# Half of the sequence rows of a Fourier mix from mirrored PSUM banks, with the mirrored input and output carried through DRAM

## The chip, the cores and the metric

The kernel runs on one core of a Trainium2 chip. The core has five engines, each with an instruction queue of its own that is worked off in order: TensorE (PE in the profile; its weight loads are listed as PEld), VectorE (DVE), ScalarE (ACT), GpSimd (POOL) and SyncE (SP). SP, ACT and POOL can also start DMA transfers; an instruction that starts one is shown as SPq, ACTq or POOLq. The metric is the device time of one execution in microseconds (us), as the median of several runs.

## The reference

Two parts, one after the other. The inputs are q, k and v of shape (4, 8, 768, 64), 8 memory keys and values for each head, and two MLP weights, 512x2048 and 2048x512. The result is (4, 768, 512) in fp32.

```
# attention: chunks of 32 queries see 16 keys to the left, 8 to the right and 8 memory keys
scores = scale * q_c @ concat(mem_k, k[l_start:r_end]).T
x[:, c_start:c_end] = softmax(scores) @ concat(mem_v, v[l_start:r_end])
# Fourier mix and MLP
mixed = real(fft(fft(x, axis=1), axis=2))          # over 768 rows and 512 columns
u  = x + mixed
un = (u - mean(u)) / sqrt(var(u) + 1e-6)
out = u + relu(un @ w_ch1) @ w_ch2
```

The input is real, so the real part of the two-dimensional transform has a symmetry that the change uses: `mixed[768 - r, 512 - c] = mixed[r, c]`, with indices taken modulo 768 and 512. Rows 0 and 384 are their own mirror images.

## The kernel before

**Units of work.** There are four batches. Each has four pairs of heads, 16 pairs in all (`attention(n)`, n from 0 to 15), then a Fourier stage (`first_fourier` for batch 0, `fourier(b)` for the others, both ending in `columns_of`), then an MLP in two halves of 384 rows (`mlp`). A batch's x lies in SBUF as `xsb`, six row tiles of 128 rows by 512 columns in fp32. Three batches have room for it.

**Attention.** GpSimd loads q and k (line 286), SP loads v with seven DMAs a pair (lines 299 to 305) into one of four buffers `va`. PE transposes q and k, forms scores and multiplies by v (lines 313, 351, 372); ACT does the exponentials (359); DVE divides by the sum and writes `xsb` (382 and 383, called normalisation below).

**Fourier stage.** DVE folds the input along both axes (lines 400 to 431), so that only a quarter of it, in even and odd combinations, goes through PE. The row transform is `e_rows` (line 440): four pairs (`par`, `ab`) with PSUM banks `ps`. It gives 193 row frequencies of each parity. ACT writes the high fp16 half of each to `up` (`e_up`, line 452), DVE the low half (`e_rest`, line 456). `up` holds frequencies 0 to 384. For the rows above, DVE makes a copy in reversed order, `dn` (`e_dn`, line 461). The column transform is `e_columns` (line 545): for each of six row tiles `kt`, eight matmuls into one PSUM bank `pm`, two column parities of four products each, with 128x128 weights from `up` (tiles 0 to 2) or `dn` (tiles 3 to 5) and 256 columns of the tables `cosD` and `nsinD` or `sinD`. Then for each tile DVE adds `pm` to `xsb` in place (`e_sum`, line 551) and takes mean and variance (557, 558), and ACT writes the fp16 copy `un` (563). In batches 1 to 3 SP transposes `un` by DMA into `unT` (`e_flip`, line 575); in batch 0 PE and DVE do it.

**MLP.** For each half, 16 products `ph` of four matmuls (line 596), each followed by a ReLU on ACT (603), then three row tiles `pc` of 16 matmuls (610); DVE scales and adds (`e_osb`, line 616) into `osb`, of which there are three buffers, and ACT sends it out (`e_out`, line 620).

**What sets the order.** Each piece of work is a task with an engine, an estimated cost, the tasks it comes after, and the buffers that it takes and gives back. `Plan.order` is a list scheduler: it works through time and places on each engine the first task that can start, in order of rank. MLP products rank last and are called fillers: PE takes one whenever nothing else is ready. The order that comes out is fixed in the program; the engines then run it in order with their own waits. PSUM has two banks with the tag `acc` (row transforms, column transforms and, in batch 3, a third of the MLP) and two with the tag `mlp`. A task of SP that is `loose` may be placed before one that is held up.

**DMA semaphores.** DMAs that SP and ACT issue signal eight semaphores, which the program assigns in turn. An instruction that starts a DMA waits until the earlier user of its semaphore has landed.

Of the kernel before, what the change touches and what calls it, by code (L numbers as in the profile page):

```python
# [10 lines left out]
FP32 = mybir.dt.float32  # L11
BF16 = mybir.dt.bfloat16
FP16 = mybir.dt.float16
# [18 lines left out]
def strided(src, off, dims):  # L32
    return bass.AP(tensor=src.tensor, offset=src.offset + off,
                   ap=[list(src.ap[0])] + [list(d) for d in dims])
# [105 lines left out]
def kernel(  # L140
# [49 lines left out]
    seq = [(b, pr) for b in range(B) for pr in (0, 2, 1, 3)]  # L190

    plan = Plan(dict(qs=NS, ks=NS, va=NV, kTb=NKT, qT=2, tr=1, sc=1, xa=1, e1=3,
                     xsb=3, fold=2, hl=1, up=4, dn=4, acc=2, mlp=2, un=6, unT=2, hT=1, osb=3))
    add = plan.add
    MLPS = 1000000

# [189 lines left out]
            xa[:, :, :, 0:D], zs.unsqueeze(3).to_broadcast([P, 3, 2, D]), ALU.mult)  # L386


    zy_of, pq_of, ff_of, hl_of, ps_of, up_of, pm_of, un_of, tp_of = ({} for _ in range(9))
    mu_of, unT_of, rstd_of, g_of = {}, {}, {}, {}  # L390
    mid = cpool.tile([P, 2, NST, 1], FP16)
    mid32 = cpool.tile([P, NST, 1], FP32)
    warm = cpool.tile([P, 1], FP32)
    gate = cpool.tile([P, 1], FP32)

    def e_zy(b, par, c):
# [60 lines left out]
                                up[:, 0].rearrange("p k s -> p s k"), ALU.subtract)  # L457

    def e_dn(b, par, ab):
        dn = fpool.tile([P, 2, HS], FP16, tag="dn", bufs=4, name="dn")  # L460
        nc.vector.tensor_copy(dn, rev_ap(up_of[b, par, ab][2], HS, HS, [[2 * NK, 2]]))
        up_of[b, par, ab][1] = dn

    def g_zy(par, g):
        if g == 0:
# [82 lines left out]

    def e_sum(b, kt):
        uv = xs[b][:, kt, :].rearrange("p (j c) -> p c j", c=2)  # L550
        nc.vector.tensor_tensor(uv, pm_of.pop((b, kt)), uv, ALU.add)  # L551

    def e_stats(b, kt):
        if kt == 0:
# [17 lines left out]
    def e_flip(b, kt):  # L572
        if kt == 0:
            unT_of[b] = fpool.tile([P, NDT, S], FP16, tag="unT", bufs=2, name="unT")
        nc.sync.dma_start_transpose(unT_of[b][:, :, ts(kt, P)], un_of.pop((b, kt)))

    def e_unT(b, kt):
        if kt == 0:
# [3 lines left out]
    def e_rstd(b):  # L582
        rstd_of[b] = rstd = fpool.tile([P, NST], FP32, tag="rstd", bufs=2, name="rstd")
        nc.gpsimd.tensor_scalar(rstd, mu_of[b][:, :, 1], eps, None, ALU.add)  # L584
        nc.gpsimd.tensor_tensor(rstd, rstd, mhalf, ALU.pow)


    def mtag(b, i):
        return "acc" if b == B - 1 and i % 3 == 2 else "mlp"
# [21 lines left out]
                             start=(ht == 0), stop=(ht == NHT - 1))  # L611

    def e_osb(b, sh, stl):
        st = sh * 3 + stl
        osb_of[b, st] = osb = fpool.tile([P, DM], FP32, tag="osb", bufs=3, name="osb")
        nc.vector.scalar_tensor_tensor(osb, pc_of.pop((b, sh, stl)), rstd_of[b][:, st:st + 1],  # L616
                                       xs[b][:, st, :], ALU.mult, ALU.add)

    def e_out(b, st):
        nc.scalar.dma_start(out[b, ts(st, P), :], osb_of.pop((b, st)))  # L620


    t_zero = add("DVE", 0.2, e_zero, rank=-21)
    t_table = add("ACT", 1.4, lambda: nc.scalar.activation(warm, zero, AFT.Sin), [t_zero], rank=-3)
# [169 lines left out]
    def first_fourier():  # L794
# [37 lines left out]
                                              give=(tag,))  # L832
        return columns_of(0, t_rest)

    def fourier(b):
        nrm = [[t_norm[b * HP + i, g] for i in ii for g in range(2)] for ii in ((0, 1), (2, 3))]
        t_rest = {}
        zy = {}
        ff = hi = None
        for par in range(2):  # L840
            zy[par] = [None]
            for c in range(2):
                zy[par].append(add("DVE", 0.96, lambda par=par, c=c: e_zy(b, par, c),
                                   nrm[c] + [ff, zy[par][-1]],
                                   take=("fold",) if c == 0 else ()))
            pq = add("DVE", 1.86, lambda par=par: e_pq(b, par), zy[par], take=("fold",),
                     give=("fold",))
            prev = pq
            for ab in range(2):
                ff = add("DVE", 1.1, lambda par=par, ab=ab: e_ff(b, par, ab), [pq, prev],  # L850
                         take=("fold",) if ab == 0 else (), give=("fold",) if ab == 1 else ())
                prev = ff
                hi = add("ACT", 0.85, lambda par=par, ab=ab: e_hi(b, par, ab), [ff, hi],
                         take=("hl",) if ab == 0 else ())
                lo = add("DVE", 0.96, lambda par=par, ab=ab: e_lo(b, par, ab), [hi],
                         give=("fold",) if ab == 1 else ())
                rw = add("PE", 1.95 if par == 0 and ab == 1 else 1.0,
                         lambda par=par, ab=ab: e_rows(b, par, ab), [lo, t_sines],
                         take=("acc",), give=("hl",) if ab == 1 else ())
                up = add("ACT", 0.6, lambda par=par, ab=ab: e_up(b, par, ab), [rw], take=("up",))  # L860
                t_rest[par, ab] = add("DVE", 0.6, lambda par=par, ab=ab: e_rest(b, par, ab),
                                      [up], give=("acc",))
        return columns_of(b, t_rest)

    def columns_of(b, t_rest):
        t_dn = {}
        for par in range(2):
            for ab in range(2):
                t_dn[par, ab] = add("DVE", 0.36, lambda par=par, ab=ab: e_dn(b, par, ab),
                                    [t_rest[par, ab]], take=("dn",))  # L870
        t_un = {}
        allr = list(t_rest.values())
        cols = {}

        def columns(kt):
            cols[kt] = add("PE", 0.9, lambda: e_columns(b, kt),
                           allr + [t_rows] + (list(t_dn.values()) if kt > 2 else []),
                           take=("acc",), rank=len(plan.tasks) + (15 if kt == 3 else 0),
                           give=("up",) * 4 if kt == 2 else ("dn",) * 4 if kt == 5 else ())

        sa = None
        columns(0)
        for kt in range(NST):
            if kt + 1 < NST:
                columns(kt + 1)
            su = add("DVE", 0.7, lambda kt=kt: e_sum(b, kt), [cols[kt]], give=("acc",))
            sa = add("DVE", 0.9, lambda kt=kt: e_stats(b, kt), [su, sa])
            un = add("ACT", 0.72, lambda kt=kt: e_un(b, kt), [sa], take=("un",))
            if b > 0:
                t_un[kt] = add("SP", 0.1, lambda kt=kt: e_flip(b, kt), [un, t_un.get(kt - 1)],  # L890
                               take=("unT",) if kt == 0 else (), give=("un",), moved=0.8,
                               loose=True)
                continue
            tp = add("PE", 0.26, lambda kt=kt: e_turn_u(b, kt), [un, t_idh], take=("mlp",),
                     give=("un",))
            t_un[kt] = add("DVE", 0.43, lambda kt=kt: e_unT(b, kt), [tp, t_un.get(kt - 1)],
                           take=("unT",) if kt == 0 else (), give=("mlp",))
        rs = add("POOL", 1.0, lambda: e_rstd(b), [sa])
        return t_un, rs
# [3 lines left out]
    def mlp(b, t_un, rs):  # L903
        for sh in range(2):
            relu = []
            c2 = None
            for ht in range(NHT):
                ph = add("PE", 0.65, lambda sh=sh, ht=ht: e_ch1(b, sh, ht),
                         mlp_prev + [t_un[3 * sh + i] for i in range(3)] + t_w1,
                         take=(mtag(b, ht),), give=("unT",) if sh == 1 and ht == NHT - 1 else (),  # L910
                         rank=MLPS + len(plan.tasks), filler=True)
                relu.append(add("ACT", 0.5, lambda sh=sh, ht=ht: e_relu(b, sh, ht),
                                [ph, relu[-1] if relu else None],
                                take=("hT",) if ht == 0 else (), give=(mtag(b, ht),),
                                rank=RELU(len(plan.tasks))))
            for stl in range(3):
                st = 3 * sh + stl
                for part in range(4):
                    end = part == 3
                    c2 = add("PE", 0.88, lambda sh=sh, stl=stl, part=part: e_ch2(b, sh, stl, part),  # L920
                             [relu[4 * part + 3], t_w2[part], c2], take=(mtag(b, stl),) if part == 0 else (),
                             give=("hT",) if stl == 2 and end else (),
                             rank=MLPS + len(plan.tasks), filler=True)
                os_ = add("DVE", 0.76, lambda sh=sh, stl=stl: e_osb(b, sh, stl), [c2, rs],
                          take=("osb",), 
                          give=(mtag(b, stl), "xsb") if st == NST - 1 else (mtag(b, stl),),
                          rank=RELU(len(plan.tasks)))
                mlp_prev[0] = c2
                add("ACT", 0.1, lambda st=st: e_out(b, st), [os_], give=("osb",), moved=0.9,
                    rank=RELU(len(plan.tasks)))  # L930

# [46 lines left out]
```

## Time and profile before

| what | value |
|---|---|
| median of 3 runs | 309.03 us (308.47 to 309.29) |
| the profiled execution | 308.85 us |
| its span in the trace | 307.1 us |
| PE matmul busy | 94% of the span, granted clock 1.00 |
| DVE busy | 56% |
| ACT busy | 53% |
| chain that ended last | PE 91%, DMA 2%, POOL 2%, DVE 1%, ACT 1%, issue 1% |
| column transform (line 545) on that chain | 7% |
| DMA traffic | 28.93 MB, mean 94 GB/s |

The span runs from the first to the last recorded instruction or transfer; the execution's own time includes what lies around it. The "chain that ended last" is followed back from the end: at each step to what released the instruction, or to the one before it on its engine. A row of the waits names who waited, at which line, and for whom. Row times of single matmuls overlap, since matmuls are pipelined: the rate is read from the chain, where 16 of the column transform take 1.75 us.

In time the batches overlap: the column transforms of batches 0 to 3 start at about 55, 108, 147 and 202 us. From about 210 us on, the MLP of batches 1, 2 and 3 is alone.

### The profile page before, as it was taken

Reading aid. Unit: us, or ns where it says so; the run is one execution under the profiler, and the core shown is the slowest. Engines: PE = TensorE matmul, PEld = TensorE weight load, DVE = VectorE, ACT = ScalarE, POOL = GpSimd, SP = SyncE. Lnnn points to the kernel's source line nnn. Section 1 sums busy time; section 2 is a strip of 40 time slices with the busy share of each in tenths; the row PEclk is TensorE's granted clock in tenths of the full one; section 3 lists DMA queues with packets and bytes.
Section 4 is the critical chain, followed back from the end, with each engine's and each line's share of the span. In section 5 each row is a group of like instructions: output and inputs, shape, how many; then the busy total and the mean of one; then the engine's idle time right before and its main releaser. Section 6 shows DMA issues by size and latency. Waiting matters only on the chain.

```text
span 307.1 us, 7496 instructions
## 1 busy us (share of the span) xinstructions
PE 289.5 (94%) x3148; PEld 181.5 (59%) x3148; DVE 171.2 (56%) x371; ACT 161.5 (53%) x291; POOL 40.8 (13%) x78
## 2 busy tenths in 40 slices
PE   1399999999999999999989999999999999999994
PEld 1267678866666676666756646675554554554541
DVE  7877895975397887797764399476101001001001
ACT  6656373689884666885257423743360450531710
POOL 8806421132201102000020000000200000000000
PEclk9999999999999999999999999999999999999999
DMA  6989999999944925821361011004201101001011
GB/s 114 197 171 167 204 205 196 198 204 178 193 72 91 203 45 111 136 47 40 89 137 36 2 46 59 0 19 102 86 2 40 64 2 68 34 2 71 31 36 68
DMA packets 60289, 28.93 MB, mean 94 GB/s; under 512 B 48480, under 2 KB 56672, under 8 KB 60256
## 3 DMA queue, kind: packets, MB, share of 16 engines
q1 hardware_dynamic: 47168, 11.61, 21.0%
q0 software_dynamic: 9344, 10.49, 20.8%
q10 hardware_dynamic: 3744, 6.36, 5.7%
q8 instruction: 25, 0.41, 0.5%
q14 instruction: 8, 0.07, 0.1%
HBM read 30.28 MB, written 6.29 MB: 119 GB/s over the span
## 4 chain that ended last, share of the span: by engine, by line
PE 91%; DMA 2%; POOL 2%; DVE 1%; ACT 1%; issue 1%; POOLq 0%; ACTq 0%
PE ph L596 28%; PE pc L610 27%; PE xa L372 9%; PE pm L545 7%; PE ps L440 5%; PE idle L654 5%; PE ps L534 4%; PE sc L351 3%; DMA qs<-in_q_dram 2%; PE trk L313 2%; PE trq L313 2%; DVE osb L616 1%; POOL qs L286 0%; ACT hT L603 0%; PE tp L570 0%
## 5 line engine op out<-in xcount | busy, mean ns | idle before, releaser
L603 ACT ACTIVATE hT<-ph 128x384 f16<-128x384 f32 x128 | 60.9, 492 | 63.0 <-PE ph L596 51.5
L596 PE MATMUL ph<-unT,w_sb 128*128 128x384 f16 x512 | 91.6, 326 | 2.2 <-ACT hT L603 1.1
L610 PE MATMUL pc<-w_sb,hT 128*128 128x512 f16 x384 | 86.9, 379 | 0.0
L596 PEld LDWEIGHTS <-w_sb 128*128 128x128 f16 x512 | 47.8, 97 | 36.8 <-issue 5.7
L616 DVE SCALAR_TENSOR_TENSOR osb<-pc,rstd,xsb 128x512 f32<-128x512 f32 x24 | 18.0, 749 | 82.5 <-PE pc L610 82.4
L610 PEld LDWEIGHTS <-hT 128*128 128x128 f16 x384 | 36.8, 98 | 41.2 <-issue 0.2
L359 ACT ACTIVATE e<-sc,mbias 128x384 f32<-128x384 f32 x64 | 33.8, 583 | 13.8 <-PE sc L351 11.3
L372 PEld LDWEIGHTS xa<-va,e 128*64 128x64 f32 x768 | 25.0, 137 | 7.8 <-issue 7.0
L372 PE MATMUL xa<-va,e 128*64 128x65 f32 x768 | 29.3, 226 | 0.0
L563 ACT ACTIVATE un<-xsb,mu_s 128x512 f16<-128x512 f32 x24 | 17.2, 720 | 14.9 <-DVE mu_s L558 14.8
L382 DVE RECIPROCAL zs<-xa 128x6 f32<-128x6 f32 x32 | 6.1, 191 | 25.6 <-PE xa L372 25.5
L452 ACT CAST up<-ps 128x386 f16<-128x386 f32 x16 | 9.7, 603 | 19.1 <-PE ps L440 13.5
L551 DVE TENSOR_TENSOR xsb<-pm,xsb 128x512 f32<-128x512 f32 x24 | 16.0, 675 | 4.4 <-PE pm L545 4.2
L383 DVE TENSOR_TENSOR xsb<-xa,zs 128x384 f32<-128x384 f32 x32 | 17.8, 557 | 1.1
L557 DVE BATCH_NORM_STATS2 st<-xsb 128x6 f32<-128x512 f32 x24 | 16.4, 684 | 0.5
L654 PE MATMUL idle<-dz 128*128 128x384 bf16 x71 | 15.3, 350 | 1.0 <-DVE zero L230 1.0
L322 ACT COPY qT<-trq 128x768 bf16<-128x768 bf16 x16 | 12.8, 798 | 5.6 <-PE trq L313 5.5
L286 POOL DMA_DIRECT2D ks<-in_k_dram x16 | 10.2, 635 | 35.0 <-PE trk L313 31.4
L584 POOL TENSOR_SCALAR rstd<-mu_s 128x6 f32<-128x6 f32 x4 | 1.0, 245 | 102.0 <-DVE osb L616 57.7
L313 PE MATMUL trq<-ident_b,qs 96*64 96x96 bf16 x256 | 9.4, 221 | 5.1 <-DMA qs<-in_q_dram 5.1
L286 POOL DMA_DIRECT2D qs<-in_q_dram x16 | 10.5, 659 | 25.2 <-PE trq L313 21.5
L456 DVE TENSOR_TENSOR up<-ps,up 128x386 f16<-128x386 f32 x16 | 9.6, 598 | 7.5 <-ACT up L452 7.5
(126 smaller groups left out, 343.5 us busy)
## 6 DMA issues: line engine op xcount, KB each, us to landing
va<-in_v_dram SPq DMA_DIRECT2D x32, 220.0 KB
out_dram<-osb ACTq DMA_DIRECT2D x24, 256.0 KB
w_sb<-in_moe_w_ch_dram POOLq DMA_DIRECT2D x8, 512.0 KB, 16.9
qs<-in_q_dram POOLq DMA_DIRECT2D x16, 192.0 KB, 5.7
ks<-in_k_dram POOLq DMA_DIRECT2D x16, 192.0 KB, 6.1
va<-in_mem_v_dram SPq DMA_DIRECT2D x32, 24.0 KB
va<-in_v_dram SPq DMA_DIRECT2D x32, 22.0 KB
va<-in_v_dram SPq DMA_DIRECT2D x16, 32.0 KB
```

The lines of the kernel that those rows point to most:

```text
L286: nc.gpsimd.dma_start(dst[n % NS][0:QP], src[b, 2 * pr:2 * pr + 2].rearrange("h (p j) d -> p h (j d)", j=RB))
L313: nc.tensor.transpose(out_[64 * hh:64 * hh + 64, j * w:(j + 1) * w], src[:, hh, j * D:(j + 1) * D], eye)
L359: nc.scalar.activation(e1[:, :, :, ts(half, 32)], sc[:, :, 0:6, ts(half, 32)], AFT.Exp, bias=mbias[:, half:half + 1], scale=1.0 / math.sqr ...
L372: nc.tensor.matmul(xa[64 * half:64 * half + 64, st, hh, 0:65], e1[:, hh, t6, :], v1[:, hh, 6 * g + t6, 0:65], start=True, stop=True)
L383: nc.vector.tensor_tensor(xs[b][:, 3 * g:3 * g + 3, 2 * pr * D:(2 * pr + 2) * D] .rearrange("p s (h d) -> p s h d", h=2), xa[:, :, :, 0:D] ...
L545: nc.tensor.matmul(pm[:, par, :], lhs, rhs[:, par, :], start=(im == 0), stop=(im == 3))
L563: nc.scalar.activation(un, xs[b][:, kt, :], AFT.Identity, bias=mu_of[b][:, kt, 0:1], scale=-1.0)
L596: nc.tensor.matmul(ph[:, 0:384], w1_sb[:, dt, ts(ht, P)], unT_of[b][:, dt, sh * 384:(sh + 1) * 384], start=(dt == 0), stop=(dt == NDT - 1))
L603: nc.scalar.activation(hT_of[b, sh][:, ht, :], ph_of.pop((b, sh, ht))[:, 0:384], AFT.Relu, bias=0.0, scale=-1.0)
L610: nc.tensor.matmul(pc_of[b, sh, stl], hT_of[b, sh][:, ht, ts(stl, P)], w2_sb[:, ht, :], start=(ht == 0), stop=(ht == NHT - 1))
L616: nc.vector.scalar_tensor_tensor(osb, pc_of.pop((b, sh, stl)), rstd_of[b][:, st:st + 1], xs[b][:, st, :], ALU.mult, ALU.add)
L654: nc.tensor.matmul(fill_of[0][:, 0:384], dz, strided(dz, 0, [[0, 3], [1, P]]), start=True, stop=True)
```

## The change

In batches 1, 2 and 3 only the column tiles 0, 1 and 2 (rows 0 to 383) are computed by matmuls. Row tile 3 + kt of `xsb` then holds the mirror image of tile kt: position p of it is row 768 - (128 kt + p). Position 0 of tile 3, which would be the mirror of row 0, is row 384. Batch 0 stays as it was, except that its four `dn` copies are now slices of one buffer.

- `e_dn` is gone from batches 1 to 3. The buffer of `dn`, one instead of four with four times the size, is used as `xr` there: three tiles of mirrored x.
- `e_back` writes x of tiles 3 to 5 to a DRAM scratch `x_rows` with the 64 rows of each half tile in reversed order (three DMAs on SP); `e_mirror` reads it back as `xr`, shifted by one row (four DMAs on SP). Both are `loose`. The first comes after the batch's last normalisation, the second after the first has landed.
- `e_last_row` multiplies the one row 384 into partition 0 of bank `pm` of tile 0: six matmuls with one weight column, after tile 0 has been summed.
- `e_sum` for tiles 0 to 2 leaves the bank in use. `e_sum_back` adds the same bank, read backwards along the columns, to `xr` and writes tile 3 + kt of `xsb`, in two DVE instructions: 2x255 elements and 2 elements. Only then is the bank given back.
- The tiles are summed in the order 0, 1, 3, 4, 2, 5. The MLP takes tiles in the order of SLOT: 0, 3, 4 in the first half, 5, 1, 2 in the second.
- Result tiles 3 to 5 of these batches don't go out by ACT: SP writes `osb` to a DRAM scratch `out_rows` (`e_out_rows`), waits until that has landed, and copies it from DRAM to DRAM with the rows reversed (`e_out_back`; one DMA more for row 384).

The core of the diff:

```
     def e_dn(b, par, ab):
-        dn = fpool.tile([P, 2, HS], FP16, tag="dn", bufs=4, name="dn")
+        if b not in dn_of:
+            dn_of[b] = fpool.tile([P, 4, 2, HS], FP16, tag="dn", bufs=1, name="dn")
+        dn = dn_of[b][:, 2 * par + ab]
...
+    def e_back(b):
+        for t in range(3):
+            r0 = xd[b % 2, t, 63:64, :]
+            nc.sync.dma_start(bass.AP(tensor=r0.tensor, offset=r0.offset,
+                                      ap=[[64 * DM, 2], [-DM, 64], [1, DM]]), xs[b][:, 5 - t, :])
+
+    def e_mirror(b):
+        xr_of[b] = xr = fpool.tile([P, 3, DM], FP32, tag="dn", bufs=1, name="xr")
+        xb = xd[b % 2].rearrange("t p d -> p t d")
+        nc.sync.dma_start(xr[1:65], xb[64:128])
+        nc.sync.dma_start(xr[65:128], xb[0:63])
+        nc.sync.dma_start(xr[0:1, 1:3], xb[63:64, 0:2])
+        nc.sync.dma_start(xr[0:1, 0:1], xb[63:64, 2:3])
+
+    def e_last_row(b):
+        pm = pm_of[b, 0]
+        for par in range(2):
+            todo = [(up_of[b, par, ab][0][:, part, HS:HS + 1], (cosD, nsinD)[ab])
+                    for ab in range(2 - par) for part in range(2)]
+            for i, (lhs, rhs) in enumerate(todo):
+                nc.tensor.matmul(pm[0:1, par, :], lhs, rhs[:, par, :], start=(i == 0),
+                                 stop=(i == len(todo) - 1))
+
+    def e_sum_back(b, kt):
+        pm, xr = pm_of.pop((b, kt)), xr_of[b]
+        y = xs[b][:, 3 + kt, :].rearrange("p (j c) -> p c j", c=2)
+        r = xr[:, kt, :].rearrange("p (j c) -> p c j", c=2)
+        nc.vector.tensor_tensor(y[:, :, 1:HD], strided(pm, HD - 1, [[HD - 1, 2], [-1, HD - 1]]),
+                                r[:, :, 1:HD], ALU.add)
+        nc.vector.tensor_tensor(y[:, :, 0], strided(pm, 0, [[2 * HD - 1, 2]]), r[:, :, 0],
+                                ALU.add)
...
+    SLOT = (0, 3, 4, 5, 1, 2)
...
+    def e_out_rows(b, st):
+        nc.sync.dma_start(od[b % 2, st - 3], osb_of.pop((b, st)))
+
+    def e_out_back(b, st):
+        t = st - 3
+        p0 = 1 if t == 0 else 0
+        src, r0 = od[b % 2, t, p0:P, :], S - P * t - p0
...
+        nc.sync.dma_start(bass.AP(tensor=top.tensor, offset=top.offset,
+                                  ap=[[HD, 2], [-DM, P - p0]] + half),
+                          bass.AP(tensor=src.tensor, offset=src.offset,
+                                  ap=[[HD, 2], [DM, P - p0]] + half))
+        if p0:
+            nc.sync.dma_start(out[b, HS:HS + 1, :], od[b % 2, 0, 0:1, :])
...
     def fourier(b):
+        t_x1 = add("SP", 0.4, lambda: e_back(b), [t_norm[b * HP + i, 1] for i in range(HP)],
+                   moved=2.0, loose=True)
+        t_xr[b] = add("SP", 0.4, lambda: e_mirror(b), [t_x1], take=("dn",), moved=2.0, loose=True)
...
+        kts, sa = (0, 1, 2, 3, 4, 5), None
+        if b == 0:
...
+        else:
+            kts = (0, 1, 3, 4, 2, 5)
 
         def columns(kt):
+            if b > 0 and kt > 2:
+                if kt == 3:
+                    cols[kt] = add("PE", 0.7, lambda: e_last_row(b), [t_sum[0]])
+                return
...
+            if b == 0 or kt < 3:
+                su = add("DVE", 0.7, lambda kt=kt: e_sum(b, kt), [cols[kt]],
+                         give=("acc",) if b == 0 else ())
+                t_sum[kt] = su
+                if b > 0 and kt == 0:
+                    columns(3)
+            else:
+                su = add("DVE", 0.8, lambda kt=kt: e_sum_back(b, kt - 3),
+                         [cols.get(kt), t_sum[kt - 3], t_xr[b]],
+                         give=("acc", "dn") if kt == 5 else ("acc",))
...
+                if b and st > 2:
+                    o1 = add("SP", 0.1, lambda st=st: e_out_rows(b, st), [os_], give=("osb",),
+                             moved=0.9, loose=True)
+                    add("SP", 0.1, lambda st=st: e_out_back(b, st), [o1], moved=0.9, loose=True)
+                    continue
```

## The prediction

> **What bounds the kernel now.** I read the busy shares first, then a table of stretches, then the waits of TensorE (PE), then the waits of SyncE's DMA queue (SPq), and last the timeline around batch 2's column products. Page and stretches:
>
> ```profile
> PE 289.5 (94%) x3148; PEld 181.5 (59%) x3148; DVE 171.2 (56%) x371; ACT 161.5 (53%) x291; POOL 40.8 (13%) x78
> ```
>
> ```profile
> 108.00:118.00 10.00, 10.00 (x164) 7.61 (x160) 9.19 (x18) 6.25 (x10) 0.63 (x1) 1.00 0.33 66
> ...
> 148.00:156.00 8.00, 8.00 (x61) 5.73 (x59) 6.63 (x13) 2.17 (x3) 0.00 (x0) 1.00 0.37 88
> 156.00:202.00 46.00, 44.88 (x443) 27.70 (x442) 29.41 (x55) 25.15 (x50) 1.60 (x2) 1.00 0.16 42
> ```
>
> The columns of a stretch are its length, then busy time and instructions of PE, weight loads, VectorE (DVE), ScalarE (ACT), GpSimd, then clock, DMA share and GB/s. Around the column products of batches 1 and 2 (the first two stretches) PE has not one idle tenth, at clock 1.00: the MLP of an earlier batch fills every hole. So a matmul taken out anywhere after 45 us is worth its full time, as long as nothing new makes PE wait. The 1.1 us that PE loses in the third stretch is the kind of wait to look for: PE waits for ACT.
>
> ```profile
> PE ph L596 <- ACT hT L603: 1.1, 3, 0.6
> ```
>
> ```profile
> SPq L295 <- DMA out_dram<-osb: 31.0, 3, 13.2
> SPq L304 <- DMA out_dram<-osb: 11.6, 1, 11.6
> ```
>
> (Waiter, what it waited for, us in total, times, longest.) The second of these fences matters most. SP loads V; ACT sends the results. Yet four times a V load stood up to 13 us behind an output DMA of ACT. All DMAs of SP and ACT share eight completion semaphores, dealt out round robin: a DMA is not issued before the one eight places ahead of it has landed, and SP's queue stands still meanwhile. Timeline of SP, and of ACT's issues:
>
> ```profile
> 131.07 13.62 SPq L295 DMA_DIRECT2D va<-in_v_dram  x2
> ...
> 145.15 5.62 SPq L295 DMA_DIRECT2D va<-in_v_dram  x2
> 150.81 0.31 SPq L304 DMA_DIRECT2D va<-in_mem_v_dram x1
> ```
>
> ```profile
> 148.45 0.34 ACTq L620 DMA_DIRECT2D out_dram<-osb  x1
> ```
>
> SP goes on at 144.7 and 150.8, each 2.3 to 2.4 us after an output of ACT was issued (142.39 and 148.45): that is how long a 256 KB output takes to land. Nobody felt it, since those V loads are used 10 us later or more.
>
> **What PE saves.** Batches 1 to 3 drop column products 3, 4 and 5: 3 x 8 = 24 matmuls of 256 columns each. They add six for the one row 384. So 18 fewer per batch, 54 in all. The chain shows 16 of them in 1.75 us, one every 0.109 us. The six have one-column weights, which makes them no cheaper: in this trace the one-column products of line 534 take 246 ns against 247 for full ones. 54 x 0.109 = **5.9 us** saved.
>
> The Trainium skill, page "TensorE: Matmul & The Clock Gate", section "Back-to-back issue gap", has two figures: an isolated N/2.4 + 2.5 ns (109 ns for 256 columns), and a sustained 131 ns for 512 columns, which it says replaces the first in a real kernel. The trace sides with the first: 48 products of 512 columns (line 610) take 10.45 us, 218 ns each. By the sustained figure (an estimate, a third of the way from its 81 ns for 128 columns to 131) the saving would be about 5.3 us.
>
> **DVE.** Twelve reversed copies (line 461, 0.36 us) go: -4.3 us. The nine sums of mirrored tiles read PSUM backwards: 510 elements, taken at the 0.68 us of line 551, plus a two-element instruction, at the 0.17 us of the 128x6 copy of line 416: +1.5 us. Reversal is free in SBUF (line 417: 762 reversed elements 0.95 us; line 400: 768 forward 0.96); from PSUM in fp32 no row shows it, so its bounds are 0 and a doubling, 0.7 us more for each sum. DVE is not the bound (56%), so I count only the first mirrored sum of each batch, on which PE depends; the doubling would cost 3 x 0.7 = 2 us.
>
> **What PE newly waits for.** Before, a PSUM bank came free after one sum. Now banks 0 and 1 are held until their mirrored sum, and product 2 needs bank 0. So: product 0, its sum, row 384, sum 1, mirrored sum 0, and only then product 2. As the changed program orders batch 2, with T the start of product 0 (147.5 us now): PE runs 16 column matmuls (1.75), 4 of line 610 (0.87), the six (0.66), 4 more (0.87), 4 of line 596 (0.65), and comes to product 2 at T+4.8. DVE has product 0 at T+1.07; a sum with its statistics takes 1.54 (sums start at 148.53, 150.09, 151.61), so mirrored sum 0 can start at T+4.15 and end at T+5.0: PE waits 0.2. In batch 1 PE has 0.6 us to spare (a value product, a score product and a transpose lie between), in batch 3 one.
>
> That holds if the mirrored x is there. Its write waits for the batch's last normalisation, its read for the write, and SP for the semaphores.
> - Batch 1: SP stands until 95.4 as now (the trace has that wait), loads head 11 by 100.1, writes x back, loads head 12 and reads x at 105 to 107, which lands near 111. Needed: 112.2. Cost 0; bounds 0 and 1.5, as two V loads are in flight.
> - Batch 3: the read stands behind the first reversed output of batch 1, out by about 179, and is needed near 200. Cost 0.
> - **Batch 2.** By the order in which the changed program's DMAs take their semaphores, the write stands behind the output of batch 0's row tile 3 (about 140) and the read behind that of row tile 4. The tile-4 result is on PE at T-1.8, but DVE first does the two low halves of the row transform, which end at T-1.2; the 0.75 us output sum ends at T-0.45, its DMA is issued at T-0.4 and lands 2.3 later, T+1.9. Only then does SP issue the four reads, 786 KB. A 256 KB output occupies the DMA engines 0.73 us (its queue: 5.7% of 307.1 us for 24), so 1.57 of its 2.3 are fixed: 0.34 issue + 2.2 + 1.57 = 4.1 us, landing at T+6.0. The mirrored sum ends at T+6.85, PE has waited **2.0 us**. Bounds: 0 (the output earlier by 2 us) and 4.5 (the reads as slow as the 6.1 us of a K load in the page's DMA part, the nearest slow row).
>
> **Pacing by ACT.** With fewer column matmuls between them, MLP products now run back to back while ACT still has six normalised copies (line 563, 0.72 us) to make. Two products are 8 x 0.163 = 1.30 us of PE, but two ReLUs (line 603, 0.49) and a copy are 1.70 us of ACT, and there are two PSUM banks. In batch 2 this exists already: from 156.15 to 160.72 PE runs 20 matmuls, 3.25 us of work, in 4.57. In batch 1 it is new: six products follow with four copies among them, 4 x 0.4 less the two banks' lead of 0.6: **1.0 us** (bounds 0 and 2).
>
> **Second half of batch 1's MLP.** It now starts directly behind the first half, not behind row transforms, so its second product waits for the last output sum. The trace has the like at 218.45 to 218.81: **0.4 us** (bounds 0 and 1.5).
>
> **Moved or hidden.** Nine outputs move from ACT to SP, by a scratch and back: 21 more SP issues in the MLP stages, where SP does little else but transposes that are needed 40 us later. The last reversed tile is the fourth of the last six to come out: its sum ends at 297.0 on the present times, the scratch write at 299.3; the present end needs 0.9 us after a landing, so the copy back sets the end only if it takes over 6.9 us. No row shows DRAM to DRAM; the nearest are 2.3 and 6.1. Cost 0. The Trainium skill, "DMA: Bandwidth & Descriptors", section "Anatomy of one DMA", gives 2.0 us plus bytes/436 GB/s and warns that a DRAM target is slowest to confirm; its estimate of 2.6 us would leave the end alone too.
>
> **Sum.** 308.85 (the profiled run; span 307.1) - 5.9 + 2.0 + 1.0 + 0.4 = 306.35. The median of the runs is 0.18 above the profiled one: **306.5 us**.
>
> **Rivals.** About 0.3%, 0.9 us, is what a measurement here can tell from no change: 308.1 and 309.96 are the bounds.
> - *Nothing is late* (27%): the output lands early, ACT keeps up, only the 0.2 and 0.4 remain: 309.0 - 5.9 + 0.6 = 303.7; 303.1 to 305.2. For it: DVE gets 2.8 us freer. Against it: SP's 42 us behind outputs.
> - *Forecast* (45%): 305.2 to 308.1.
> - *The losses eat the gain* (14%): 308.1 to 309.96; reads at their 4.5 bound and pacing at 2 leave 309.03 - 5.9 + 4.5 + 2 + 0.4 = 310.0 at the very end of it.
> - *Slower* (14%): x's way through DRAM, behind semaphores, holds product 2 in more than one batch. With 1.4 for the rest it decides from 5.4 us of such waits: 4.5 in batch 2 and 1.5 in batch 1 give 6.0, so 310.5. For it: every DMA of SP inherits ACT's delays. Against: batch 3 has 20 us of room.
> - That the change saves no work is excluded by the instruction count; that the saving lies off the path, by the stretches with PE full.
>
> The range, 303.6 to 309.8, leaves out some of the first and the last case. Faster 27 + 45 = 72%, same 14%, slower 14%.
>
> **What would show it.** PE: 138 matmuls at the column line, not 192, and 5.9 us less of them on the chain. Waits: a new row of PE at the column line behind DVE, about 2 us, and of DVE's mirrored sum behind a DMA in batch 2; more of PE behind ACT's ReLU, 2 us instead of 1.1. SP: the read of the mirrored rows of batch 2 issued 2 to 2.5 us after an output. Wrong would be: mirrored sums over 1 us, a wait in batches 1 or 3, or an end set by SP's last copy.

## The result and the profile after

The changed kernel takes 360.53 us (360.01 to 360.95, four runs) where the kernel before takes 309.16 (308.47 to 309.58) beside it: 1.1663 of the time, 95% interval 1.1634 to 1.1692. The forecast was 306.5, with a range of 303.6 to 309.8. It missed by 54 us and had the wrong sign. Medians here and below are of all executions, while the ratios leave out single executions in a slower state, so that the two can differ by 0.3%.

From the page of the changed kernel, its busy line, the clock of TensorE by slices, and the first line of its chain:

```profile
PE 292.7 (81%) x3094; PEld 178.4 (50%) x3094; DVE 168.1 (47%) x368; ACT 161.7 (45%) x291; POOL 40.7 (11%) x78
...
PEclk9999999999999756999955999999969999999998
...
PE 71%; DMA 12%; DVE 7%; SPq 5%; issue 2%; ACT 2%; DVEq 0%; ACTq 0%
```

The 54 matmuls are gone (3148 to 3094), yet TensorE is busy for longer than before, 292.7 us, because the clock falls in three places. TensorE holds 71% of the chain instead of 91%; DMA, DVE and SP's queue have what it lost. The waits of TensorE and VectorE in the changed kernel (waiter, what it waited for, us in total, times, longest):

```profile
PE pm L581 <- DVE xsb L497: 38.8, 2, 21.4
PE ph L637 <- DVE osb L657: 4.9, 2, 4.7
...
PE ph L637 <- ACT hT L644: 3.4, 7, 0.6
```

```profile
DVE xsb L495 <- DMA xr<-x_rows: 39.7, 2, 22.3
...
DVE osb L657 <- DMA out_dram<-osb: 15.2, 3, 6.4
```

Line 581 is the column transform, 497 the second instruction of the mirrored sum. TensorE stands twice, 38.8 us in all, ahead of product 2, because the mirrored sum stands for the mirrored x. The chain of waits around batch 1, and then around batch 2 (start, length, what):

```profile
109.71 1.85 PE pm L581 x16
...
115.55 3.49 SPq L299
...
128.41 0.60 SPq L477
...
130.30 5.75 DMA xr<-x_rows
136.16 0.69 DVE xsb L495
...
136.97 1.89 PE pm L581 x8
```

```profile
164.51 2.04 DMA out_dram<-osb
...
166.62 0.56 SPq L471
...
167.80 18.51 DMA x_rows<-xsb
...
186.46 0.65 SPq L477
...
188.38 4.54 DMA xr<-x_rows
```

In batch 2 the write of x is 768 KB and lands 18.51 us after its last issue; the read takes 4.54 more. Before it there is a release by an output of ScalarE. In batch 1 TensorE stands from 115.55 to 136.97, and SP comes to the read at 128.41 only. Its eight matmuls then take 1.89 us, where sixteen took 1.85 at 109.71: half speed. The stretches show the clock (length, busy time and instructions of PE, weight loads, DVE, ACT and POOL, then clock, DMA share, GB/s):

```profile
113.00:123.00 10.00, 2.54 (x38) 1.33 (x36) 0.86 (x2) 3.11 (x6) 0.63 (x1) 0.87 0.40 86
123.00:133.00 10.00, 0.00 (x0) 0.00 (x0) 0.00 (x0) 0.00 (x0) 0.00 (x0) 0.50 0.41 124
133.00:143.00 10.00, 6.03 (x64) 3.41 (x65) 6.59 (x15) 2.90 (x5) 0.00 (x0) 0.60 0.61 130
143.00:153.00 10.00, 10.00 (x140) 6.37 (x139) 6.07 (x14) 8.72 (x19) 1.61 (x2) 1.00 0.61 125
```

So a stall is paid twice: once as idle time, and once more in the matmuls after it. The rest of the loss is in the MLP stage. Here are the chain at two outputs of ScalarE, and the DMA engines in the stretch of 252 to 262 us, cut in 40 (busy share in tenths, and GB/s):

```profile
253.47 7.09 DMA out_dram<-osb
...
260.66 0.76 DVE osb L657
```

```profile
349.09 6.20 DMA out_dram<-osb
```

```profile
DMA  2001111399911111111011111111499995000099
GB/s 20 16 25 37 45 41 49 93 249 297 88 49 49 45 49 49 37 49 41 33 49 45 41 45 45 49 50 45 75 297 438 239 254 112 0 0 0 33 369 385
```

These two outputs of 256 KB take 7.09 and 6.20 us, where one took 2.3 before. After a first hump of up to 297 GB/s the engines run for over four microseconds at one tenth and 33 to 50 GB/s: a copy back from scratch (issued at 250.67) in two halves is under way. `osb` has three buffers, so the next sum waits for that output, and TensorE 4.7 us for the sum. At the end of the kernel VectorE waits for the other. The trace also has the times of the 16 semaphore updates that tell of an output's landing. For the output at 349.09 fourteen came within 1.99 us and the last two after 5.28 and 6.20, so that two parts of sixteen were late. For the one at 253.47 all came late, after 5.07 to 7.09 us; two DMA transposes were in flight as well, and why all sixteen were held is not shown.

The Trainium skill, "DMA: Bandwidth & Descriptors", section "Why a DMA increments its semaphore by 16 and not by 1", under "How many engines (k)", has the rule that I overlooked: a transfer is spread over the largest number of engines, up to 16, that divides the slowest dimension of both of its sides. By it the three writes of x and the copies back (slowest dimension 2 on the DRAM side) run on two engines of 16. This trace agrees, by the one tenth of the share and the 33 to 50 GB/s. Its count of semaphore updates for a landing fits too: 16 for an output of ScalarE, 3 for each write of x and each copy back of a tile, and in the runs below 5 and 9 for the write in four and eight blocks, one more than the slowest dimension of 2, 4 and 8. Worked out by that rule from the prediction's 0.73 us of 16 engines for 256 KB, an estimate for the writes is 3 x 0.73 x 16/2 = 17.5 us, beside the 18.51 of the chain. The rule spoke against this change before the run.

### The profile page after: what moved, and what is told of

It reads as the page before. It is cut to its first block, busy times and chain, and to the rows that moved or that the text cites. A ratio compares the mean times of both kernels' runs of the same rounds, so it can differ in the third digit from the quotient of the medians.

```text
span 359.2 us, 7432 instructions
## 1 busy us (share of the span) xinstructions
PE 292.7 (81%) x3094; PEld 178.4 (50%) x3094; DVE 168.1 (47%) x368; ACT 161.7 (45%) x291; POOL 40.7 (11%) x78
## 4 chain that ended last, share of the span: by engine, by line
PE 71%; DMA 12%; DVE 7%; SPq 5%; issue 2%; ACT 2%; DVEq 0%; ACTq 0%
PE ph L637 25%; PE pc L651 18%; PE xa L372 8%; DMA x_rows<-xsb 5%; DMA out_dram<-osb 4%; PE idle L710 4%; PE pm L581 4%; PE ps L442 4%; PE ps L570 3%; DMA xr<-x_rows 3%; PE sc L351 3%; SPq L295 2%; PE trk L313 2%; PE trq L313 2%; DVE osb L657 1%
## 5 line engine op out<-in xcount | busy, mean ns | idle before, releaser
L637 PE MATMUL ph<-unT,w_sb 128*128 128x384 f16 x512 | 97.1, 339 | 9.0 <-DVE osb L657 4.9
L637 PEld LDWEIGHTS <-w_sb 128*128 128x128 f16 x512 | 49.6, 101 | 47.6 <-issue 19.1
L581 PE MATMUL pm<-cosD,up 128*128 128x256 f16 x48 | 10.2, 297 | 38.8 <-DVE xsb L497 38.8
L581 PEld LDWEIGHTS <-up 128*128 128x128 f16 x96 | 9.7, 105 | 42.0 <-DVE xsb L497 39.6
L495 DVE TENSOR_TENSOR xsb<-pm,xr 128x510 f32<-128x510 f32 x9 | 6.1, 677 | 39.8 <-DMA xr<-x_rows 39.7
L427 ACT CAST hi<-ff 128x768 f16<-128x768 f32 x12 | 9.7, 832 | 11.7 <-DVE ff L419 11.6
```

Source lines behind the costliest of these rows:

```text
L581: nc.tensor.matmul(pm[:, par, :], lhs, rhs[:, par, :], start=(im == 0), stop=(im == 3))
L637: nc.tensor.matmul(ph[:, 0:384], w1_sb[:, dt, ts(ht, P)], unT_of[b][:, dt, sh * 384:(sh + 1) * 384], start=(dt == 0), stop=(dt == NDT - 1))
```

## The experiments

Each run is named by what it edits; its time is a median, set against the kernel before on the same chip. Theory A: the transfers are long, since they use few engines. Theory B: the order is wrong; the scheduler was told 2.0 us for each of the two transfers of x, and so put product 2 where x isn't yet there. Theory C: the transfers start late, since they stand in SP's queue behind ScalarE's outputs and loads of V. A rival to all three is that the arithmetic itself is slower than I worked out.

### Arithmetic alone

```
-        t_x1 = add("SP", 0.4, lambda: e_back(b), ...)
-        t_xr[b] = add("SP", 0.4, lambda: e_mirror(b), [t_x1], ...)
+        t_xr[b] = None
...
-        r = xr[:, kt, :].rearrange("p (j c) -> p c j", c=2)
+        r = y
...
-                if b and st > 2:
+                if False:
```

> This kernel keeps the halved column transform, the held PSUM banks, the row 384 and the two-instruction mirrored sums, but leaves out both ways through DRAM: tiles 3 to 5 add their own x instead of the mirrored one, and go out by ACT in storage order, so they come out unmirrored. Theory A (the loss of 51 us is all in the transfers, which run on two of the sixteen DMA engines because the outermost dimension of their DRAM side has size 2): about 305 to 307 us, the saving of 5.9 less 1 to 3 us of waits for ACT. Theory B (holding the banks until the mirrored sums stalls PE whatever the transfers do): above 312 us, with PE waiting at the column line for DVE.

Measured: 305.55 us, 0.9855 of before (0.9835 to 0.9874), clock 0.998. The rival is out: the products, the backward sums and the new order of the tiles are worth 4.5 us. All that follows is in the two ways through DRAM.

### The write of x in eight blocks, and in four

```
-                                      ap=[[64 * DM, 2], [-DM, 64], [1, DM]]), xs[b][:, 5 - t, :])
+                                      ap=[[BS * DM, P // BS], [-DM, BS], [1, DM]]),
...
-        nc.sync.dma_start(xr[1:65], xb[64:128])
-        nc.sync.dma_start(xr[65:128], xb[0:63])
+        for r in range(BS, P, BS):
+            nc.sync.dma_start(xr[P + 1 - r - BS:P + 1 - r], xb[r:r + BS])
+        for r in range(0, BS, 16):
+            n = min(16, BS - 1 - r)
+            nc.sync.dma_start(xr[P + 1 - BS + r:P + 1 - BS + r + n], xb[r:r + n])
```

With BS = 16 (eight blocks):

> Only the way of x is changed: rows are reversed in blocks of 16 instead of 64, so the write to DRAM has an outermost dimension of 8, and the read back fetches the blocks in reversed order with ten DMAs instead of four. Output path as in the change. Theory A (engines per transfer): the three writes land within 5 us of the first issue instead of about 20, PE's wait at the column line falls from 38.8 us to under 8, the time to 316 to 324 us. Theory C (SP's queue standing behind ACT's outputs is what makes x late): SP still waits as long, the time stays above 350. Theory D (a write to DRAM followed by a read is that slow however it is split): stays near 360.

With BS = 32 (four blocks):

> The same with blocks of 32: outermost dimension 4, six DMAs read back. Theory A: the writes run at twice the rate of the change and half that of blocks of 16, some 100 GB/s, and land about 9 to 10 us after the first issue; PE's wait at the column line about 16 to 22 us, the time 333 to 343 us, between the other two. Theories C and D: no such step, above 350.

Measured: 345.61 us (ratio 1.1156, 1.1098 to 1.1215) with eight and 349.92 (1.1276, 1.123 to 1.1322) with four. VectorE's wait for the mirrored x falls with the number of blocks, 39.7, 27.5 and 17.6 us for two, four and eight, so the number of engines counts, but the times are 22 and 7 us above the upper end of what theory A gave. (The four-block run reads back with seven DMAs, not six as expected.) In the chain of the run with eight blocks, at batch 2:

```profile
158.53 5.33 DMA out_dram<-osb
163.95 0.33 SPq L481
...
167.12 3.17 DMA xr<-x_rows
```

The write was issued at 154.3 and is no longer what is late. The read (line 481) stands behind an output of ScalarE that takes 5.33 us to land. This is the coupling that the prediction named for batch 2, with an output of 5.33 us in place of 2.3. Theory A alone doesn't carry the loss.

### The outputs in pieces of 16 rows

```
-        nc.sync.dma_start(od[b % 2, st - 3], osb_of.pop((b, st)))
+        r0 = od[b % 2, st - 3, 15:16, :]
+        nc.sync.dma_start(bass.AP(tensor=r0.tensor, offset=r0.offset,
+                                  ap=[[16 * DM, 8], [-DM, 16], [1, DM]]), osb_of.pop((b, st)))
...
-                                  ap=[[HD, 2], [-DM, P - p0]] + half),
+                                      ap=[[DM, ni], [-16 * DM, na], [1, DM]]),
```

(`ni` is 16 and `na` is 8; in tile 3 the piece that holds row 384 is moved apart.)

> Only the way of the outputs is changed: the scratch write reverses blocks of 16 (outermost dimension 8), and the copy from DRAM to DRAM has an outermost dimension of 16. x as in the change. Theory A: the wait of DVE's output sum for a free buffer (15.2 us in three places, 6.4 of it at the very end) goes, with what PE lost behind it: 348 to 352 us. Theory C: no change at the end of the kernel, 358 to 361.

Measured: 346.54 us (1.1175, 1.1154 to 1.1195), 14.0 us less than the change and a little better than expected. The wait of the output sums on ScalarE's outputs, 15.2 us, is gone, and that for the mirrored x is unchanged at 39.7. So the copies in two halves held ScalarE's outputs back.

### Both edits

The two edits above together, x in eight blocks.

> Both edits of the two runs before together: the mirrored x is written in eight blocks of 16 rows and read in ten pieces, and each output goes to scratch in eight blocks and comes back in sixteen. If the two losses are separate, the gains add: 360.5 - 14.9 - 14.0 = 331.6 us (328 to 336), with the wait for the mirrored x still near 17.6 us and no wait of the output buffers left. If the outputs of the eight-block run were what made its x late (they share SP's queue and the DMA engines with it), the wait for the mirrored x falls under 10 us as well and the time to 318 to 326. If the length of the transfers is all there is, 306 to 312.

Measured: 326.63 us (1.0537, 1.0486 to 1.0587), 34 us less than the change where the two gains make 29. So the losses are separate in the main, with 5 us more saved than the two gains add up to. 21 us over the arithmetic alone remain, and they are in the wait for x, as the next run shows.

### Both edits, with the scheduler told 6 and 8 us

```
-                   moved=2.0, loose=True)
-        t_xr[b] = add("SP", 0.4, lambda: e_mirror(b), [t_x1], take=("dn",), moved=2.0, loose=True)
+                   moved=6.0, loose=True)
+        t_xr[b] = add("SP", 0.4, lambda: e_mirror(b), [t_x1], take=("dn",), moved=8.0, loose=True)
```

> The kernel with both edits, and the planner is told 6.0 us for the write of x and 8.0 us for its read (in place of 2.0 and 2.0), about what the eight-block run showed. Nothing else is edited; the planner then puts other products ahead of the second and third mirrored product. Theory of the order (the loss is that TensorE and VectorE stand in line behind a sum whose operand isn't there, while MLP matmuls that could run are queued after it): the wait for the mirrored x falls under 5 us and the time is 308 to 320. Theory of the length (there is no other work at that point, or the transfers cross the outputs wherever they stand): within 5 us of the run with both edits alone.

Measured: 326.79 us (1.0571, 1.0522 to 1.0621): no change, and TensorE still waits 19.4 us at the column line. Taken alone, this is what the theory of the length expects. My reading is another, and the last run below bears on it: the length of the transfers is not all that the scheduler has to know; it reckons without SP's stops. The waits of SP's queue in this run:

```profile
SPq L473 <- DMA out_dram<-osb: 13.5, 1, 13.5
SPq L304 <- DMA out_dram<-osb: 11.8, 2, 10.6
...
SPq L295 <- DMA out_dram<-osb: 7.6, 1, 7.6
```

Line 473 is the write of x in this kernel; its 13.5 us are ahead of batch 2's, issued at 155.19. Lines 304 and 295 are loads of V. The write of batch 1 was issued at 106.76, as in the change.

### Two halves as in the change, with the scheduler told 20 and 6 us

The same two numbers in the changed kernel, 20.0 and 6.0, nothing else.

> The changed kernel with its transfers on two engines as they are, and the planner told 20.0 us for the write of x and 6.0 us for its read. Theory of the order: the 38.8 us that TensorE waits ahead of the mirrored product fall under 12 us, since MLP work of the batch before is put there, and the time is 322 to 338; what is left is the outputs' part (mid and tail waits, 11 us) and lower clock. Theory of the length: a slow transfer on SP's queue holds whatever is behind it (the transposes of the next tiles, the outputs), so the wait turns up at another line and the time stays over 345.

Measured: 330.29 us (1.067, 1.0619 to 1.072), 30 us less than the change, with the same slow transfers. The waits of TensorE in this run, and then SP's queue around batch 1's write:

```profile
PE xa L372 <- DMA va<-in_mem_v_dram: 8.8, 2, 8.2
...
PE pm L581 <- DVE xsb L497: 3.3, 2, 2.2
```

```profile
106.56 5.22 SPq L471 DMA_DIRECT2D x_rows<-xsb  x3
111.89 7.30 SPq L299 DMA_DIRECT2D va<-in_v_dram  x1
```

Theory B holds in part: 38.8 us become 3.3, as attention, MLP products and the next fold now run in the gap. Theory A's objection is seen too, at a smaller size: the load of V behind the write takes 7.30 us to issue, and TensorE stands 8.2 us, to 129.34, for a load of V.

### The mirrored x alone, in eight blocks and in two

`if b and st > 2:` becomes `if False:`, so the outputs leave by ScalarE; x in eight blocks:

> The mirrored x through scratch in eight blocks of 16 rows, and the outputs of the mirrored rows written by ScalarE's queue in the order they have (so they land in the wrong rows: the reversal of the outputs is left out). Set beside the eight-block run (345.6 us) this is what the outputs cost there, beside the arithmetic alone (305.6 us) what x costs. If the outputs' waits add to those of x: 345.6 - 12.6 = 333 us (329 to 337). If the copies back were also what slowed the ReLUs and x: 318 to 328. If x is nearly all of the loss: 338 to 345.

And x in two halves as in the change:

> The changed kernel with x through scratch in two halves on SP's queue as it is, and the outputs of the mirrored rows written by ScalarE's queue in the order they have (their reversal is left out). If the losses are separate: 360.5 less 14.0 (the outputs' edit alone) = 346.5 us or up to 3 below, as no copy back shares the engines. If the copies back are what slowed x too, under 335.

Measured: 327.88 us (1.0593, 1.0564 to 1.0623) and 347.12 (1.1224, 1.1192 to 1.1257). The second is where separate losses put it. The first is just inside the band in which copies back slow more than the outputs: beside x in eight blocks the outputs' way cost 17.7 us (345.61 less 327.88), where their waits had been 12.6. In the second, the waits are the change's:

```profile
PE pm L581 <- DVE xsb L497: 38.2, 2, 21.3
```

### The outputs alone, in two halves

`t_xr[b] = None` and `r = y` as in the arithmetic alone; the outputs as in the change.

> The arithmetic of the change and the outputs' way through scratch in two halves; the mirrored product is added to x of its own rows and the transfer of x is left out. Beside the arithmetic alone (305.6 us) this is the price of the outputs' way by itself. If the losses of x and of the outputs are separate: 305.6 + 7 to 14 = 313 to 320 us (7.4 is what the outputs' edit gave with x on GpSimd's queue, 14.0 what it gave in the changed kernel). If the outputs only cost where x shares SP's queue with them, 305 to 309.

Measured: 312.83 us (1.0119, 1.0088 to 1.0149). TensorE's waits and VectorE's:

```profile
PE ph L637 <- DVE osb L657: 2.6, 4, 2.0
```

```profile
DVE osb L657 <- DMA out_dram<-osb: 16.3, 3, 6.5
```

The account in ratios to the kernel before: arithmetic 0.9855 - 1 = -0.0145; x alone 1.1224 - 0.9855 = 0.1369; outputs alone 1.0119 - 0.9855 = 0.0264; the change as a whole has 1.1663 - 1 = 0.1663, so 0.0175 is left for their meeting. Of 309 us that is -4.5, +42, +8 and +5. The four intervals leave the last about 2 us either way. The loss is mainly the way of x, and nearly a sum.

### The mirrored x on GpSimd's queue

```
-            nc.sync.dma_start(bass.AP(tensor=r0.tensor, offset=r0.offset,
+            nc.gpsimd.dma_start(bass.AP(tensor=r0.tensor, offset=r0.offset,
...
-        nc.sync.dma_start(xr[1:65], xb[64:128])
+        nc.gpsimd.dma_start(xr[1:65], xb[64:128])
...
-        t_xr[b] = add("SP", 0.4, ...)
+        t_xr[b] = add("POOL", 4.8, ...)
```

(All four reads, and the write's task in the same way, with 3.0.)

> The changed kernel with one thing moved: the write of x to scratch and the reads of its mirror are issued by GpSimd's queue, in the same two halves; outputs as in the changed kernel. In the trace of the changed kernel SP's queue stands 11.0 and 7.6 us behind outputs of ScalarE before it comes to the write of batch 1's x (x is ready at 84, the write is issued at 107). Theory of the place in SP's queue: issued at 85 to 88, even a write of 18.5 us and a read of 5 land by 113, where the first mirrored sum stands; the wait for the mirrored x falls from 39.7 us to under 12, and the time is 322 to 334, with the outputs' 11 us left in. Theory of the engine count (two halves stay on two engines in any queue): the read waits for the write on GpSimd's queue, the next keys queue behind it, TensorE waits for keys instead, and the time stays over 340.

Measured: 319.24 us (1.0276, 1.0203 to 1.035), 41 us less than the change, and 3 better than expected. GpSimd's queue:

```profile
84.92 2.46 POOL L471 DMA_DIRECT2D x_rows<-xsb  x3
99.23 0.63 POOL L477 DMA_DIRECT2D xr<-x_rows  x1 [11.18 <-DMA x_rows<-xsb]
```

VectorE's whole wait for x is 0.8 us. The write of batch 1 is issued at 84.92, so x had been ready 22 us before SP came to it in the change. From the write to the read it is 14.3, 18.3 and 14.1 us in the three batches here. In the change it is 19.8 in batch 2 (166.62 to 186.46) and 18.4 in batch 3, so the run moves two things. But 84.92 + 19.8, four issues of the read (2.5) and its 5.75 us make 113.0, and the first mirrored sum stands at 114.53 here. For batch 1 the earlier issue is enough by itself. In batch 2 the write is issued at 126.78; the same sum gives 154.8, and the first mirrored sum, which has the 0.8 us of waiting ahead of it, stands at 153.50. So there the earlier issue accounts for all but some 1.3 us, by this estimate.

What is left of the loss sits in SP's queue again. TensorE waits once for a transposed tile of batch 1's MLP:

```profile
PE ph L637 <- DMA unT<-un: 5.8, 1, 5.8
```

The transpose is issued at about 156, after SP has stood for an output of ScalarE that takes 6.28 us to land (148.01 to 154.29).

### The same with the outputs in pieces, and x in blocks as well

The run above with the outputs' edit:

> The run with x on GpSimd's queue, and the outputs' way through scratch in pieces of 16 besides. The outputs' edit was worth 14 us alone (360.5 to 346.5) and 19 us beside the eight-block x (345.6 to 326.6). If the two losses are separate it is worth 11 to 15 us here as well: 308 to 320, if x's move is worth what the theory of the place in the queue says; 326 to 332 if it is not.

And with x in eight blocks on that queue besides:

> As the run with x on GpSimd's queue and the outputs in pieces of 16, with x in eight blocks and ten reads on that queue. If the shape counts on GpSimd's queue as it does on SP's, this is 5 to 20 us faster than the one with two halves on that queue: 304 to 314. If GpSimd's queue cuts the transfers in its own way, the same within 2 us, or slower by the six reads more in each batch (4 us of issue each).

Measured: 311.80 us (1.0049, 1.0017 to 1.0081) and 306.07 (0.9898, 0.9846 to 0.9951). The outputs' edit is worth 7.4 us here, less than the 11 to 15 expected. In blocks, it is 10.2 us from the write to the read (85.33 to 95.49), not 14.3. The page of the last run:

```profile
PE 285.3 (94%) x3094; PEld 176.0 (58%) x3094; DVE 168.4 (55%) x368; ACT 161.2 (53%) x291; POOL 62.1 (20%) x117
...
PEclk9999999999999999999999999999999999999998
```

TensorE waits nowhere for x or for an output buffer, and the clock never falls. This version does the whole computation and takes less than both kernels: 1.0% less than before. It is near where the arithmetic alone stands (0.9855), so both ways through DRAM are then nearly free. That also rules out a theory D of the expectations, that a write to DRAM followed by a read is slow however it is split.

### All on SP's queue, in pieces, with the scheduler told 20 and 6 us

> Both transfers in eight and sixteen pieces on SP's queue, and the planner told 20.0 us for the write and 6.0 us for the read, as in the run of the prices alone (330.3 us). Theory of the order: the waits for the mirrored x (22 us with both edits) and those of the outputs (11 us with the prices alone) both go, and the time is 306 to 313. If SP's semaphores hold the queue whatever the order, 316 to 324.

Measured: 318.49 us (1.0296, 1.0231 to 1.036), the second of the two cases. SP still stands 8.2 us behind an output of ScalarE at a write of x, and TensorE waits 3.8 at the column line, where it waited 19.4 when the scheduler was told 6 and 8 us. So the order takes away 8 us and most of that wait, but not the stops of SP. 14 us over the arithmetic alone remain (1.0296 against 0.9855), and this run doesn't show where they all are.

## Why the prediction was wrong

**The step that failed** is the one that begins "That holds if the mirrored x is there". Its terms were 0, 2.0 and 0 us for batches 1, 2 and 3; TensorE waited 21.4, 17.4 and 0. Within it:

- *The transfer was mis-sized.* I priced 768 KB of x like ScalarE's outputs, "A 256 KB output occupies the DMA engines 0.73 us". An output has 128 rows on both sides; the scratch has two half tiles, and its write landed 18.51 us after the last issue. The diff shows the shape `[[64 * DM, 2], ...]`; I read it for its order and not for its spread. This is the larger part: with the write at 107.13 the read came 21.3 us later, where the prediction had 7 at most (100.1 to 107).
- *Batch 1's start.* The text put the first stop of SP at 95.4 and the read at 105 to 107. The stop was there (11.0 us, to 95.9), but a second one of 7.6 us followed, again behind an output; the write was issued at 107.13, the read at 128.41. The waits of SP's queue in the changed kernel between 60 and 112 us:

```profile
SPq L304 <- DMA out_dram<-osb: 11.0, 1, 11.0
SPq L295 <- DMA out_dram<-osb: 7.6, 1, 7.6
```

- *Batch 2's start.* That the batch stands behind outputs was right: the write was released by one at 166.6, and its 19.8 us to the read are the loss. (The upper bound of 4.5 us for this batch is 4.1 to 4.4 by the prediction's own numbers.) In the run with eight blocks, where the write is short, the read stands behind one, as forecast.
- *Batch 3* has no wait for x, as forecast.

**The second failed step** is "Cost 0" for the outputs' way. I looked for SP's last copy to set the end, if it took over 6.9 us. It did take longer: issued at 347.65, it landed 8.75 us later. The 2.6 us that the prediction worked out for it did not hold; the figure behind them is for DMAs that GpSimd issues, and this one is SP's. Yet the copy doesn't set the end: outputs of ScalarE, which share the engines with such copies, land in 6 to 7 us instead of 2.3, and three buffers of `osb` turn that into a wait at 261 and at the end. Alone it costs 2.6% (8 us).

**What neither step had**: the lower clock after each stall. TensorE's busy time is 292.7 us with the change and 284.4 with the arithmetic alone, for the same matmuls: 8 us.

**What was right.** With the terms for x set aside the prediction's sum is -5.9 + 1.0 + 0.4 = -4.5 us; the arithmetic alone measured -4.5. That they agree so well is in part luck, since the parts are not all as told: in that run TensorE waits less for ScalarE than before (0.6 us, 1.1 before), not more, but 2.2 us for a transposed copy, a row that before didn't have. The column matmuls are 138, as forecast (120 at line 581 and 18 at line 488 for row 384). The mirrored sum, reversed from PSUM, takes 677 ns, where I took 680 and kept a doubling as a bound. ScalarE's pacing in the change is 3.4 us of waits where before had 1.1; 2 was forecast.

**The rivals.** The one that came is the last, x's way through DRAM holding product 2 in more than one batch. Its mechanism, its place and its point of decision, 5.4 us, were right; its price of 6.0 us was far too low, since its bound for the reads was a K load and the write had no bound of its own.

**What stays open.** The three theories are not exclusive: more engines (-15 us), another order (-30) and another queue (-41) each took away part of the same loss in the change. The queue counts most here, but that run has a faster write as well; the sums under it make the place in the queue nearly enough, as an estimate. Why GpSimd's queue is faster with the same write, and where the last 14 us of the run with everything on SP's queue are, stays open.

## What to carry to other kernels

Before pricing a transfer by a row of the trace, compare the outermost dimension on both sides with that row's: three writes of 256 KB took 19.8 us here, where an output of 256 KB had taken 2.3, and one side of them began with a 2. Ask of every added transfer when its queue will come to it, not only when its data are ready: x waited 22 us in SP's queue, 18.6 of them for outputs of another engine. A list order computed from assumed times needs the measured ones, the queue's stops included, or it puts the consumer where it can only wait.

## What the runs showed of the hardware

- Reading PSUM backwards in fp32 costs VectorE nothing that the rows show: 510 elements reversed take 677 ns, against 670 ns for the forward sum of 512 (line 587).
- A slow transfer holds the queue that issued it: the issue of a load of V that takes 0.6 us of SP took 6.5 us in the change and 7.3 with the scheduler told 20 and 6 us, behind the two-engine write. It also holds others' transfers: outputs of ScalarE of 256 KB that met a two-engine copy went from 2.3 to 6 or 7 us.
- In the two long stalls of the change, by stretches of 1 us, the granted clock falls to 0.50 within 2 to 5 us after TensorE stops (115.5 to 120.5, and 176.4 to 178.5). It is back at 1.00 some 4 and 5 us after TensorE goes on (136.97 to 141, and 193.81 to 199); until then matmuls run at half speed.
- GpSimd's queue was done with the same write in two halves sooner than SP's: 14.3, 18.3 and 14.1 us from the write to the read, against 19.8 and 18.4.
